# One store from four partitions, two engines for the last copy, and the last 64 KB of a weight spread by row counts of 123, 3 and 2

## The chip, the cores and the metric

The kernel runs on one core of one Trainium2 chip. The metric is the device time of one execution in microseconds (us). Most executions of one kernel lie within 0.3% of each other, which here is 0.6 us.

## The reference, cut to what matters

```python
# B=4 batches, one new token, D=512; 32 query heads over 8 key/value heads, head size 128, window 4096
q = x @ wq
o = softmax(q k^T / sqrt(128)) v        # over the last 4096 cached keys of each batch and head
a = o.reshape(4, 1, 4096) @ wo          # wo: 4096 x 512
b = ((relu(x W_gate)) * (x W_up)) @ W_down
return g * a + (1 - g) * b              # g = sigmoid(sum(x * gate_w)); result 4 x 1 x 512, bf16
```

Some 81 MB are read (key and value caches 67 MB, weights the rest) for a result of 4 KB. The order of the loads is q weights, caches, gate and up weights, the last value block, down weight, and last the output weight `wo` (4 MB).

## The kernel before

Everything is loaded by DMAs (transfers by the core's 16 DMA engines) issued from SyncE (SP). TensorE (PE) multiplies matrices and leaves its sums in PSUM; VectorE (DVE) and ScalarE (ACT) copy and work element by element. A "set" is one of the eight blocks of keys and values. The output weight comes in six pieces; `wo` row 32p+i lies in partition p, so piece (lo, hi) is a 128-row load with (hi-lo) KB in each partition. The two 256-column halves ("column tiles", j) of the result are accumulated in partitions 0-3 and 64-67 of one PSUM bank.

```python
WO_PIECES = ((0, 8), (8, 16), (16, 24), (24, 28), (28, 30), (30, 32))
OUTT = 2; OW = 512 // OUTT; OR = 128 // OUTT          # 2 tiles, 256 columns, 64 partitions apart
...
def store(E, e, t):                                   # t=0 on SP, t=1 on ACT
    E.op(lambda: e.dma_start(out...[:, OW * t:OW * t + OW], osum[OR * t:OR * t + 4, :]), waits=[("OSUM",)], ...)
...
def OQ(g):          # once after set 4, once at the end: folds the attention output into oq
    ...             # 16 matmuls of 128 columns
def WO(p):
    lo, hi = WO_PIECES[p]
    for i in range(lo, hi):
        for j in range(OUTT):
            mm(banks[ACC][OR * j:OR * j + 4, 0:OW], oq[:, i, :], Wo[:, i, OW * j:OW * j + OW], ...)
...
def FIN():          # DVE alone, both halves in one copy of 128 partitions
    E.op(lambda: v.tensor_copy(osum[:, :], banks[ACC][:, 0:OW]), ev=("OSUM",), waits=[last piece done])
```

Of the kernel before, what the change touches and what calls it, by code (L numbers as in the profile page):

```python
# [19 lines left out]
NSET = 8  # L20
# [3 lines left out]
BIG = 1.0e30  # L24
WO_PIECES = ((0, 8), (8, 16), (16, 24), (24, 28), (28, 30), (30, 32))
OUTT = 2
OW = 512 // OUTT
OR = 128 // OUTT

class _Plan:  # L30
# [71 lines left out]
def _alloc(nc, ctx):  # L102
    R = {}

    def sb(name, shape, dt):
        R[name] = ctx.enter_context(nc.sbuf_tensor(name, shape, dt))

    sb("slots", [128, NSLOT, 16384], BF16)
    sb("kt", [128, 4, 4096], BF16)
    sb("sc", [128, 2048], BF16)  # L110
    sb("pe", [128, 2048], BF16)
    sb("pT", [128, 2, 2048], BF16)
    sb("qblk", [128, NSET, 2, 144, 2], BF16)
    sb("xsb", [4, 512], BF16)
    sb("xT", [128, 16], BF16)
    sb("gwT", [128, 4], BF16)
    sb("osb", [128, 4, 512], BF16)
    sb("oq", [128, 32, 4], BF16)
    sb("identb", [128, 128], BF16)
    sb("identf", [128, 128], FP32)  # L120
    sb("ones", [128, 128], FP32)
    sb("ee", [16, 128], FP32)
    sb("e4", [16, 128], FP32)
    sb("rfold", [128, 128], FP32)
    sb("grpb", [128, 128], BF16)
    sb("own8", [128, 8], FP32)
    sb("scl", [128, 8], FP32)
    sb("maskl", [128, 128], BF16)
    sb("maskr", [128, 512], BF16)
    sb("maskf", [128, 512], BF16)  # L130
    sb("gwB", [128, 4, 128], BF16)
    sb("fold", [128, 4, 4, 64], BF16)
    sb("mx4", [128, 4], FP32)
    sb("rd32", [128, 8, 4], BF16)
    sb("negmax", [128, 2], FP32)
    sb("rowsum", [128, NSET], FP32)
    sb("recip", [128, 2, 4], FP32)
    sb("ge", [128, 2, 4], FP32)
    sb("gp", [128, 2, 4], FP32)
    sb("gg", [128, 2, 4], FP32)  # L140
    sb("hg", [128, 14, 4], BF16)
    sb("osum", [128, OW], BF16)
    R["psum"] = ctx.enter_context(nc.psum_tensor("bank", [128, 8, 512], FP32))
    return R


def _order():
    o = [("CONST", k) for k in ("mask", "grp", "rfold")] + [("XT",), ("Z",), ("Q",), ("QT",), ("KT", 0, 0), ("KT", 0, 1), ("SC", 0, 0)]
    o += [("KT", 0, 2), ("SC", 0, 1), ("KT", 0, 3), ("SC", 0, 2)]
    for s in range(1, NSET):  # L150
        o += [("KT", s, 0), ("SC", s - 1, 3)] + [("RS", 0), ("OQ", 0)] * (s == 5) + [("SW", s - 1)]
        o += [("KT", s, 1), ("PT", s - 1), ("SC", s, 0), ("KT", s, 2), ("SC", s, 1), ("KT", s, 3)]
        o += [("SC", s, 2)] + [("PV", s - 1)] * (s < NSET - 1)
    s = NSET - 1
    o += [("SC", s, 3), ("SW", s), ("PV", s - 1), ("PT", s), ("RS", 1), ("GU",), ("PV", s), ("FFN",), ("OQ", 1)]
    return o + [("WO", p) for p in range(len(WO_PIECES))]

# [29 lines left out]
def _program(nc, plan, R, aps):  # L187
# [19 lines left out]
    Wd = slot("wd")[:, 0:14 * 512]  # L207
    Wo = slot("wo", 0).rearrange("p (i c) -> p i c", i=32)
    grelu, hrow, hT = sc[:, 0:448], sc[:, 512:960], sc[:, 1024:1472]
# [28 lines left out]
    def sc_free(key):  # L238
        n = scf[key] - NSC
        return [("E",) + sck[n]] if n >= 0 else [("INIT",)]  # L240

    def set_of(s):
        return s % 4, s // 4

    def ob(s):
        return banks[OB[s % 2]]

    def store(E, e, t):
        E.op(lambda: e.dma_start(out.rearrange("b o d -> (b o) d")[:, OW * t:OW * t + OW], osum[OR * t:OR * t + 4, :]),
             ev=("OUT", t), waits=[("OSUM",)], ctr=f"d_out{t}")  # L250

    def sync(e):
# [5 lines left out]
        for it in _dma_order():  # L258
# [15 lines left out]
            elif k == "wo":  # L274
                lo, hi = WO_PIECES[it[1]]
                load(("WO", it[1]), f"d_wo{it[1]}", Wo[:, lo:hi, :], A_wo.rearrange("(p i) c -> p i c", i=32)[:, lo:hi, :],
                     waits=w)
            else:
# [3 lines left out]
                     waits=w)  # L282
        for t in range(0, OUTT, 2):
            store(E, e, t)
        E.wait([("OUT", t) for t in range(OUTT)])

# [29 lines left out]
    def tensor(t):  # L316
# [77 lines left out]

        def OQ(g):
            key = ("OQ", g)
            r = 64 * g
            for t in range(2):
                for cc in range(2):
                    for c in range(4):  # L400
                        x = 256 * t + 128 * cc + 32 * c
                        first, lastmm = (t, cc, c) == (0, 0, 0), (t, cc, c) == (1, 1, 3)
                        mm(banks[tr(key)][r:r + 64, 0:128], R["fold"][:, 2 * cc + t, c, :], osb[:, :, x:x + 32], first,
                           lastmm, ev=key if lastmm else None, pos=(0, r),
                           waits=tr_free(key) + [("NORM", 4 * g + 3), ("FOLD", 7)] if first else ())

# [18 lines left out]
        def WO(p):  # L425
            lo, hi = WO_PIECES[p]
            w = [("WO", p)] + [("E", "OQ", g) for g in range(2)]
            for i in range(lo, hi):
                for j in range(OUTT):
                    mm(banks[ACC][OR * j:OR * j + 4, 0:OW], oq[:, i, :], Wo[:, i, OW * j:OW * j + OW], False, i == 31,  # L430
                       ev=("WOP", p) if (i, j) == (hi - 1, OUTT - 1) else None, waits=w if (i, j) == (lo, 0) else (),
                       pos=(0, OR * j))

# [6 lines left out]
    for it in order:  # L440
# [27 lines left out]
        elif k == "PV":  # L468
            act.append(("NORM", it[1]))
        elif k == "OQ":  # L470
            dve.append(("EOQ", it[1]))
    dve.append(("FIN",))

    def qd(n):
# [8 lines left out]
    def vector(v):  # L483
# [62 lines left out]
        def ERS(g):  # L546
            key = ("RS", g)
            E.op(lambda: v.reciprocal(recip[:, 0, :], banks[tr(key)][:, 0:4]), ev=("E",) + key, waits=[key])
            E.op(lambda: v.tensor_tensor(recip[:, 1, :], recip[:, 0, :], gg[:, 0, :], ALU.mult), ev=("RG", g),
                 waits=[("E",) + key, ("G",)])  # L550

        def EOQ(g):
            key = ("OQ", g)
            r = slice(64 * g, 64 * g + 64)
            E.op(lambda: v.tensor_tensor(oq[r, :, :].rearrange("p i b -> p b i"),  # L555
                                         banks[tr(key)][r, 0:128].rearrange("p (b i) -> p b i", b=4),
                                         bc(recip[r, 1, :].unsqueeze(2), 2, 32), ALU.mult), ev=("E",) + key,
                 waits=[key, ("RG", g)])

# [15 lines left out]
        def FIN():  # L575
            E.op(lambda: v.tensor_copy(osum[:, :], banks[ACC][:, 0:OW]), ev=("OSUM",), waits=[("WOP", len(WO_PIECES) - 1)])  # L576

# [5 lines left out]
    def scalar(a):  # L583
# [17 lines left out]
        def NORM(s):  # L601
            E.op(lambda: a.activation(osb[:, s % 4, :], ob(s), ACTF.Copy), ev=("NORM", s),  # L602
                 waits=[("PV", s)] + ([("OQ", 0)] if s >= 4 else []))

# [14 lines left out]

        fns = dict(ECONST=ECONST, GWB=GWB, EQ=EQ, GE=GE, RELU=RELU, EXP=EXP, NORM=NORM)  # L620
        for it in act:
            fns[it[0]](*it[1:])
        for t in range(1, OUTT, 2):
            store(E, a, t)

# [29 lines left out]
```

## Time and profile before

| | before |
|---|---|
| median time | 197.36 us (197.16 to 197.44, 3 runs) |
| span of the profiled run | 195.59 us |
| bytes read, share of the 16 DMA engines in use | 81.01 MB, 97.1% |
| last piece of `wo` landed | 192.84 us after the span's start |
| last matmul ended, DVE copy ended | 193.27, 193.74 |
| stores issued / landed | 193.77 (both) / 194.94 (SP), 195.13 (ACT) |

From the page of the kernel before: the DMA queues with packets, MB and the share of 16 engines' span. Queue q1 carries the kernel's loads; the two "instruction" queues fetch the program itself.

```profile
q1 hardware_dynamic: 3904, 81.01, 97.1%
q8 instruction: 6, 0.10, 0.2%
q14 instruction: 1, 0.01, 0.0%
```

The loads alone fill the span, and the engines' work before the tail is hidden behind them. What is left is the tail. The chain that ended last, of the kernel before, in order of time (start, duration, what):

```profile
173.35 19.49 DMA slots<-in_A_wo_dram
192.84 0.04 issue
192.89 0.40 PE bank L320 x4
193.29 0.02 issue
193.31 0.42 DVE osum L576
```

The last piece lands at 192.84; after it come four matmuls, a DVE copy and the stores. The timeline of the kernel before shows the end (start, duration, engine, line, operation; in brackets the idle time before it and what ended it):

```profile
192.89 0.38 PE L320 MATMUL bank<-slots,oq 128*4 128x256 bf16 x4 [0.24 <-DMA slots<-in_A_wo_dram]
193.31 0.42 DVE L576 CAST osum<-bank 128x256 bf16<-128x256 f32 x1 [6.46 <-PE bank L320]
193.77 0.29 SPq L249 DMA_DIRECT2D out_dram<-osum  x1
193.77 0.62 ACTq L249 DMA_DIRECT2D out_dram<-osum  x1
```

One more thing must be read, and no summary line shows it. A 16-engine DMA adds 1 to its semaphore for each engine that has finished its share, so the trace holds 16 completion times for every load. For the kernel before, sorted, and split where the sorted list has its gap:

```
load ending near    early engines   late engines   last early, last late completion (us)
   51.5                  15              1
   70.9                  14              2
   80.6                  13              3
  119.5                  12              4
  148.6                  11              5
  183.4                  10              6          184.00, 185.34
  191.0 (last piece)     10              6          191.55, 192.84
16 KB instruction packets start at: 39.08, 72.01, 110.93, 146.00, 182.58 (and 191.52); an 8 KB one at 63.71
```

(A load is named by its first completion.) The number of late engines goes up by one after each instruction packet, except the last (191.52), behind which no more of the loads come.

The packet times show the delay themselves. A 16 KB packet takes 0.92 to 1.06 us, the 8 KB one 0.31 us. Behind each of the six before 191 us, a packet of a load begins 7 to 16 ns before the end of the instruction packet and is slow: 1.71 to 1.87 us for 32 KB instead of 1.21, and in the last case 0.81 us for 8 KB instead of 0.31. The packet and the slowness behind it make a delay of 1.4 to 1.6 us for each 16 KB and of 0.97 us for the 8 KB (sums from these times). The late engines stay behind to the end (the first of them 0.87 us after the last early one in the last piece): every load gives each engine the same share again. All 16 engines must finish a load, so the six late ones set the end: 192.84, where ten engines were done by 191.55. The Trainium skill, "Runtime: NRT & Kernel Launch", section "Instruction fetch mechanics", says that an engine's program is refilled in blocks of 16 KiB by DMA; the packets of 16384 bytes agree, the one of 8192 bytes is left unexplained.

### The profile page before, as it was taken

How to read it: one execution, taken by the hardware profiler on the slowest of the kernel's cores; microseconds unless marked ns; L12 is line 12 of the kernel's file. 1: busy time of each engine (PE TensorE's matmuls, PEld its weight loads, DVE VectorE, ACT ScalarE, POOL GpSimd, SP SyncE). 2: the span in 40 equal slices, each digit the busy share in tenths (PEclk: the TensorE clock that was granted, in tenths of full speed). 3: DMA queues.
4: the chain of work that ended last, by engine and by line, in shares of the span. 5: the costliest groups of instructions: out<-in, count | busy, mean ns of one | idle time of the engine just before them, and what ended most of it. 6: DMA issues, size and time to landing. Idle time of an engine off the chain costs nothing.

```text
span 195.6 us, 1780 instructions
## 1 busy us (share of the span) xinstructions
PE 121.2 (62%) x741; PEld 50.9 (26%) x741; DVE 124.0 (63%) x153; ACT 27.3 (14%) x33; POOL 9.5 (5%) x25
## 2 busy tenths in 40 slices
PE   0418279465933894595468953893395557734954
PEld 0213123122411331142113521241141112412631
DVE  6104769999299819971998199819972997460000
ACT  2213000040130013001300131014001400420100
POOL 7830000000000000000000000000000000000000
PEclk9999957999999697999886999699999789997999
DMA  6999999999999999999999999999999999999991
GB/s 221 442 423 436 429 442 436 419 436 429 436 456 429 437 426 436 429 429 429 436 429 436 426 429 429 429 429 429 429 426 429 429 405 434 448 429 403 417 402 53
DMA packets 3919, 81.12 MB, mean 415 GB/s; under 512 B 572, under 2 KB 584, under 8 KB 968
## 3 DMA queue, kind: packets, MB, share of 16 engines
q1 hardware_dynamic: 3904, 81.01, 97.1%
q8 instruction: 6, 0.10, 0.2%
q14 instruction: 1, 0.01, 0.0%
q10 hardware_dynamic: 8, 0.00, 0.0%
HBM read 81.01 MB, written 0.00 MB: 414 GB/s over the span
## 4 chain that ended last, share of the span: by engine, by line
DMA 54%; DVE 30%; PE 9%; issue 5%; SPq 1%; ACT 0%
DMA slots<-in_A_k_cache_dram 38%; DVE kt L492 21%; DMA slots<-in_A_wo_dram 10%; PE bank L320 7%; DMA gwT<-in_gate_w_dram 6%; DVE sc L528 5%; DVE qblk L518 1%; SPq L256 1%; DVE pT L543 1%; PE bank L324 1%; DVE rd L532 1%; ACT gwB L598 0%; DVE negmax L538 0%; DVE oq L555 0%; DVE osum L576 0%
## 5 line engine op out<-in xcount | busy, mean ns | idle before, releaser
L492 DVE STREAM_TRANSPOSE kt<-slots 128x2048 f32<-128x2048 f32 x32 | 73.7, 2304 | 27.5 <-DMA slots<-in_A_k_cache_dram 27.5
L320 PE MATMUL bank<-kt,qblk 128*128 128x512 bf16 x256 | 71.4, 430 | 29.2 <-DVE kt L492 29.1
L320 PEld LDWEIGHTS bank<-kt,qblk 128*128 128x128 bf16 x256 | 24.9, 106 | 70.7 <-DVE kt L492 37.6
L320 PE MATMUL bank<-slots,pT 128*64 128x512 bf16 x256 | 32.0, 407 | 5.7 <-DMA slots<-in_A_v_cache_dram 5.7
L617 ACT ACTIVATE pe<-sc,negmax 128x2048 bf16<-128x2048 bf16 x8 | 16.0, 2002 | 60.3 <-DVE negmax L538 60.3
L528 DVE CUSTOM_DVE_ANT_0 sc<-bank,maskf 128x512 bf16<-128x512 f32 x32 | 21.1, 658 | 4.1 <-PE bank L320 4.1
L320 PEld LDWEIGHTS bank<-slots,pT 128*64 128x64 bf16 x256 | 15.0, 117 | 23.1 <-issue 13.1
L543 DVE STREAM_TRANSPOSE pT<-pe 128x2048 bf16<-128x2048 bf16 x8 | 18.5, 2312 | 2.2 <-ACT pe L617 2.2
L602 ACT ACTIVATE osb<-bank 128x512 bf16<-128x512 f32 x8 | 4.8, 597 | 81.5 <-PE bank L320 81.5
L320 PE MATMUL bank<-rd,grpb 128*128 128x32 bf16 x8 | 1.5, 192 | 21.0 <-DVE rd L532 19.3
L555 DVE TENSOR_TENSOR oq<-bank,recip 64x128 bf16<-64x128 f32 x2 | 0.9, 442 | 11.5 <-PE bank L320 11.4
L320 PEld LDWEIGHTS bank<-rd,grpb 128*128 128x128 bf16 x8 | 0.8, 97 | 24.7 <-DVE rd L532 22.7
L320 PE MATMUL bank<-slots,oq 128*4 128x256 bf16 x64 | 4.3, 272 | 2.6 <-DMA slots<-in_A_wo_dram 1.9
L496 DVE COPY xT<-bank 128x16 bf16<-128x16 bf16 x1 | 0.2, 167 | 8.2 <-PE bank L324 8.2
L320 PE MATMUL bank<-slots,xT 128*4 128x512 bf16 (+1 forms) x64 | 5.2, 483 | 0.0
L576 DVE CAST osum<-bank 128x256 bf16<-128x256 f32 x1 | 0.4, 425 | 6.5 <-PE bank L320 6.5
L518 DVE TENSOR_SCALAR qblk<-bank 32x64 uint32<-32x64 uint32 x16 | 2.9, 215 | 2.3 <-PE bank L324 2.2
L320 PE MATMUL bank<-maskr,maskl 128*128 128x512 bf16 x1 | 0.6, 609 | 5.9 <-POOL maskr L296 5.9
L324 PE MATMUL bank<-identb,xsb 4*128 4x4 bf16 x4 | 0.3, 166 | 5.4 <-DMA xsb<-in_A_x_dram 5.4
L320 PEld LDWEIGHTS bank<-slots,oq 128*4 128x4 bf16 x64 | 2.3, 83 | 4.4 <-DMA slots<-in_A_wo_dram 3.1
L296 POOL TENSOR_SCALAR_AFFINE_SELECT fold<-fold 128x256 bf16<-128x256 bf16 x8 | 3.3, 417 | 1.1
L487 DVE MEMSET qblk<- 128x2304 uint32 x1 | 2.0, 1978 | 1.4 <-PEq L640 1.4
(58 smaller groups left out, 42.2 us busy)
## 6 DMA issues: line engine op xcount, KB each, us to landing
slots<-in_A_k_cache_dram SPq DMA_DIRECT2D x8, 4096.0 KB, 25.2
slots<-in_A_v_cache_dram SPq DMA_DIRECT2D x8, 4096.0 KB, 30.6
slots<-in_A_wq_dram SPq DMA_DIRECT2D x1, 4096.0 KB, 12.4
slots<-in_A_wo_dram SPq DMA_DIRECT2D x3, 1024.0 KB, 16.4
slots<-in_B_W_gate_dram SPq DMA_DIRECT2D x1, 1792.0 KB, 19.7
slots<-in_B_W_up_dram SPq DMA_DIRECT2D x1, 1792.0 KB, 23.6
slots<-in_B_W_down_dram SPq DMA_DIRECT2D x1, 1792.0 KB, 18.6
slots<-in_A_wo_dram SPq DMA_DIRECT2D x1, 512.0 KB, 19.2
```

The lines of the kernel that those rows point to most:

```text
L256: E.op(lambda: e.dma_start(dst, src), ev=ev, waits=waits, ctr=ctr)
L296: op(lambda: e.affine_select(dst, src, pattern, cmp, fill, base=base, channel_multiplier=mult), ev)
L320: E.op(lambda: t.matmul(out_, lhsT, rhs, start=start, stop=stop, tile_position=pos, skip_group_check=True), ev=ev, waits=waits)
L324: E.op(lambda: t.transpose(out_, in_, idn), ev=ev, waits=waits)
L487: E.op(lambda: v.memset(qblk[:, :, :, :, :].rearrange("p s h c e -> p (s h c e)"), 0.0), ev=("QZ",))
L492: E.op(lambda: v.transpose(kt[:, f, :].bitcast(FP32), slot("k", s)[:, 4096 * f:4096 * f + 4096].bitcast(FP32)), ev=("E", "KT", s, f), waits=w)
L518: E.op(lambda dst=dst, r=r, g=g: v.tensor_scalar(dst, src[r, g, 0:B, :, :], 0, None, op0=ALU.bitwise_or), ev=("E",) + keys[1] if (q, g) == ...
L528: E.op(lambda: v.tensor_tensor_reduce(sc[:, 512 * f:512 * f + 512], banks[scb(key)], R["maskf"][:, :], 1.0, -3.0e38, ALU.add, ALU.max, mx4 ...
L532: E.op(lambda: v.tensor_tensor(rd32[:, :, :], bc(R["own8"][:, :].unsqueeze(2), 2, 4), bc(mx4[:, :].unsqueeze(1), 1, 8), ALU.mult), ev=("MA ...
L543: E.op(lambda: v.transpose(pT[:, s % 2, :], pe[:, :]), ev=("E", "PT", s), waits=[("EXP", s)] + ([("PV", s - 2)] if s >= 2 else []))
L602: E.op(lambda: a.activation(osb[:, s % 4, :], ob(s), ACTF.Copy), ev=("NORM", s), waits=[("PV", s)] + ([("OQ", 0)] if s >= 4 else []))
L617: E.op(lambda: a.activation(pe[:, :], sc[:, :], ACTF.Exp, bias=negmax[:, s % 2:s % 2 + 1], scale=SCALE, accum_out=rowsum[:, s:s + 1]), ev= ...
```

## The change

The intent: take work off the tail. (1) The last 64 KB of `wo` (one of 64 half-rows of 512 bytes per partition) are loaded as three row groups of 123, 3 and 2 partitions. The Trainium skill, "DMA: Bandwidth & Descriptors", section "Why a DMA increments its semaphore by 16 and not by 1", says that a DMA runs on the largest number k of engines, up to 16, that divides its slowest dimension, and on the lowest-numbered k. So 123 = 3 x 41 rows go to engines 0 to 2, and so do the 3; the 2 rows go to engines 0 and 1. (2) ACT copies the first half of the result while DVE copies the second, both into partitions 0 to 3, and one store from SP replaces two. (3) The two OQ halves are merged into one at the end. (Two small constant matmuls also become bf16.)

```diff
-WO_PIECES = ((0, 8), (8, 16), (16, 24), (24, 28), (28, 30), (30, 32))
+WO_PIECES = ((0, 16), (16, 32), (32, 48), (48, 56), (56, 60), (60, 63), (63, 64))     # now in half-rows
+LOW3 = (0, 123, 126, 128)
...
-    sb("osb", [128, 4, 512], BF16)
+    sb("osb", [128, NSET, 512], BF16)
-    sb("osum", [128, OW], BF16)
+    sb("osum", [4, 512], BF16)
...
-        o += ... [("RS", 0), ("OQ", 0)] * (s == 5) ...        # OQ in two halves
+        o += ... [("RS", 0)] * (s == 5) ...                   # OQ once, at the end, 16 matmuls of 256 columns
...
-        store(E, e, t)                                         # one on SP, one on ACT
+        load(("OUT",), "d_out", out..., osum[:, :], waits=[("OSUM", 0), ("OSUM", 1)])
...
+    def wo_rows(p):
+        return [slice(a, b) for a, b in zip(LOW3, LOW3[1:])] if p == len(WO_PIECES) - 1 else [slice(0, 128)]
+                for n, r in enumerate(wo_rows(it[1])):
+                    load(("WO", it[1], n), f"d_wo{it[1]}", Wo[r, OW * lo:OW * hi], wo[r, OW * lo:OW * hi], waits=w)
...
         def FIN():     # DVE
-            v.tensor_copy(osum[:, :], banks[ACC][:, 0:OW])     # after the last piece
+            v.tensor_copy(osum[:, OW:2 * OW], banks[ACC][OR:OR + 4, 0:OW])        # after the last piece
+        def FIN():     # ACT
+            a.activation(osum[:, 0:OW], banks[ACC][0:4, 0:OW], ACTF.Copy)         # after the last but one
```

More of the change, by code (lines that the diff above doesn't have):

```diff
@@ L121, in _alloc @@
     sb("ones", [128, 128], FP32)
-    sb("ee", [16, 128], FP32)
-    sb("e4", [16, 128], FP32)
+    sb("ee", [16, 128], BF16)
+    sb("e4", [16, 128], BF16)
     sb("rfold", [128, 128], FP32)
@@ L136, in _alloc @@
     sb("rowsum", [128, NSET], FP32)
-    sb("recip", [128, 2, 4], FP32)
+    sb("recip", [128, 4, 4], FP32)
     sb("ge", [128, 2, 4], FP32)
@@ L150, in _order @@
     for s in range(1, NSET):
-        o += [("KT", s, 0), ("SC", s - 1, 3)] + [("RS", 0), ("OQ", 0)] * (s == 5) + [("SW", s - 1)]
+        o += [("KT", s, 0), ("SC", s - 1, 3)] + [("RS", 0)] * (s == 5) + [("SW", s - 1)]
         o += [("KT", s, 1), ("PT", s - 1), ("SC", s, 0), ("KT", s, 2), ("SC", s, 1), ("KT", s, 3)]
@@ L154, in _order @@
     s = NSET - 1
-    o += [("SC", s, 3), ("SW", s), ("PV", s - 1), ("PT", s), ("RS", 1), ("GU",), ("PV", s), ("FFN",), ("OQ", 1)]
+    o += [("SC", s, 3), ("SW", s), ("PV", s - 1), ("PT", s), ("RS", 1), ("GU",), ("PV", s), ("FFN",), ("OQ",)]
     return o + [("WO", p) for p in range(len(WO_PIECES))]
@@ L207, in _program @@
     Wd = slot("wd")[:, 0:14 * 512]
-    Wo = slot("wo", 0).rearrange("p (i c) -> p i c", i=32)
+    Wo = slot("wo", 0)
     grelu, hrow, hT = sc[:, 0:448], sc[:, 512:960], sc[:, 1024:1472]
@@ L246, in ob @@
         return banks[OB[s % 2]]
-    def store(E, e, t):
-        E.op(lambda: e.dma_start(out.rearrange("b o d -> (b o) d")[:, OW * t:OW * t + OW], osum[OR * t:OR * t + 4, :]),
-             ev=("OUT", t), waits=[("OSUM",)], ctr=f"d_out{t}")
     def sync(e):
@@ L275, in sync @@
                 lo, hi = WO_PIECES[it[1]]
-                load(("WO", it[1]), f"d_wo{it[1]}", Wo[:, lo:hi, :], A_wo.rearrange("(p i) c -> p i c", i=32)[:, lo:hi, :],
-                     waits=w)
+                wo = A_wo.rearrange("(p i) c -> p (i c)", i=32)
+                for n, r in enumerate(wo_rows(it[1])):
+                    load(("WO", it[1], n), f"d_wo{it[1]}", Wo[r, OW * lo:OW * hi], wo[r, OW * lo:OW * hi], waits=w)
             else:
@@ L282, in sync @@
                      waits=w)
-        for t in range(0, OUTT, 2):
-            store(E, e, t)
-        E.wait([("OUT", t) for t in range(OUTT)])
+        load(("OUT",), "d_out", out.rearrange("b o d -> (b o) d"), osum[:, :], waits=[("OSUM", 0), ("OSUM", 1)])
+        E.wait([("OUT",)])
     def gpsimd(e):
@@ L393, in PV, with OQ @@
                        (f, c) in ((3, 12), (3, 14)), ev=("PV", s) if (f, c) == (3, 14) else None, waits=w, pos=(0, r))
-        def OQ(g):
-            key = ("OQ", g)
-            r = 64 * g
+        def OQ():
+            key = ("OQ",)
             for t in range(2):
@@ L402, in OQ @@
                         first, lastmm = (t, cc, c) == (0, 0, 0), (t, cc, c) == (1, 1, 3)
-                        mm(banks[tr(key)][r:r + 64, 0:128], R["fold"][:, 2 * cc + t, c, :], osb[:, :, x:x + 32], first,
-                           lastmm, ev=key if lastmm else None, pos=(0, r),
-                           waits=tr_free(key) + [("NORM", 4 * g + 3), ("FOLD", 7)] if first else ())
+                        mm(banks[tr(key)][0:64, 0:256], R["fold"][:, 2 * cc + t, c, :], osb[:, :, x:x + 32], first, lastmm,
+                           ev=key if lastmm else None, pos=(0, 0),
+                           waits=tr_free(key) + [("NORM", NSET - 1), ("FOLD", 7)] if first else ())
         def GU():
@@ L426, in WO @@
             lo, hi = WO_PIECES[p]
-            w = [("WO", p)] + [("E", "OQ", g) for g in range(2)]
-            for i in range(lo, hi):
-                for j in range(OUTT):
-                    mm(banks[ACC][OR * j:OR * j + 4, 0:OW], oq[:, i, :], Wo[:, i, OW * j:OW * j + OW], False, i == 31,
-                       ev=("WOP", p) if (i, j) == (hi - 1, OUTT - 1) else None, waits=w if (i, j) == (lo, 0) else (),
-                       pos=(0, OR * j))
+            w = [("WO", p, n) for n in range(len(wo_rows(p)))] + [("E", "OQ")]
+            for x in range(lo, hi):
+                i, j = x // OUTT, x % OUTT
+                mm(banks[ACC][OR * j:OR * j + 4, 0:OW], oq[:, i, :], Wo[:, OW * x:OW * x + OW], False, i == 31,
+                   ev=("WOP", p) if x == hi - 1 else None, waits=w if x == lo else (), pos=(0, OR * j))
         fns = dict(CONST=CONST, XT=XT, Z=Z, Q=Q, QT=QT, SC=SC, PV=PV, SW=SW, RS=RS, OQ=OQ, WO=WO, GU=GU, FFN=FFN)
@@ L470, in _program @@
         elif k == "OQ":
-            dve.append(("EOQ", it[1]))
+            dve.append(("EOQ",))
     dve.append(("FIN",))
+    act.append(("FIN",))
     def qd(n):
@@ L547, in ERS, with EOQ @@
             key = ("RS", g)
-            E.op(lambda: v.reciprocal(recip[:, 0, :], banks[tr(key)][:, 0:4]), ev=("E",) + key, waits=[key])
-            E.op(lambda: v.tensor_tensor(recip[:, 1, :], recip[:, 0, :], gg[:, 0, :], ALU.mult), ev=("RG", g),
+            E.op(lambda: v.reciprocal(recip[:, 2 * g, :], banks[tr(key)][:, 0:4]), ev=("E",) + key, waits=[key])
+            E.op(lambda: v.tensor_tensor(recip[:, 2 * g + 1, :], recip[:, 2 * g, :], gg[:, 0, :], ALU.mult), ev=("RG", g),
                  waits=[("E",) + key, ("G",)])
-        def EOQ(g):
-            key = ("OQ", g)
-            r = slice(64 * g, 64 * g + 64)
-            E.op(lambda: v.tensor_tensor(oq[r, :, :].rearrange("p i b -> p b i"),
-                                         banks[tr(key)][r, 0:128].rearrange("p (b i) -> p b i", b=4),
-                                         bc(recip[r, 1, :].unsqueeze(2), 2, 32), ALU.mult), ev=("E",) + key,
-                 waits=[key, ("RG", g)])
+        def EOQ():
+            key = ("OQ",)
+            for g in range(2):
+                r = slice(64 * g, 64 * g + 64)
+                E.op(lambda g=g, r=r: v.tensor_tensor(
+                    oq[r, :, :].rearrange("p i b -> p b i"),
+                    banks[tr(key)][0:64, 128 * g:128 * g + 128].rearrange("p (b i) -> p b i", b=4),
+                    bc(recip[0:64, 2 * g + 1, :].unsqueeze(2), 2, 32), ALU.mult), ev=("E",) + key if g else None,
+                    waits=[key, ("RG", 1)])
         def H():
@@ L575, in FIN @@
         def FIN():
-            E.op(lambda: v.tensor_copy(osum[:, :], banks[ACC][:, 0:OW]), ev=("OSUM",), waits=[("WOP", len(WO_PIECES) - 1)])
+            E.op(lambda: v.tensor_copy(osum[:, OW:2 * OW], banks[ACC][OR:OR + 4, 0:OW]), ev=("OSUM", 1),
+                 waits=[("WOP", len(WO_PIECES) - 1)])
         fns = dict(INIT=INIT, EKT=EKT, EXT=EXT, EQ=EQ, G=G, EQT=EQT, ESC=ESC, MAX=MAX, ESW=ESW, EPT=EPT, ERS=ERS, EOQ=EOQ, H=H,
@@ L601, in NORM @@
         def NORM(s):
-            E.op(lambda: a.activation(osb[:, s % 4, :], ob(s), ACTF.Copy), ev=("NORM", s),
-                 waits=[("PV", s)] + ([("OQ", 0)] if s >= 4 else []))
+            E.op(lambda: a.activation(osb[:, s, :], ob(s), ACTF.Copy), ev=("NORM", s),
+                 waits=[("PV", s)])
         def GE():
@@ L618, in EXP @@
                                       accum_out=rowsum[:, s:s + 1]), ev=("EXP", s), waits=w)
-        fns = dict(ECONST=ECONST, GWB=GWB, EQ=EQ, GE=GE, RELU=RELU, EXP=EXP, NORM=NORM)
+        def FIN():
+            E.op(lambda: a.activation(osum[:, 0:OW], banks[ACC][0:4, 0:OW], ACTF.Copy), ev=("OSUM", 0),
+                 waits=[("WOP", len(WO_PIECES) - 2)])
+        fns = dict(ECONST=ECONST, GWB=GWB, EQ=EQ, GE=GE, RELU=RELU, EXP=EXP, NORM=NORM, FIN=FIN)
         for it in act:
             fns[it[0]](*it[1:])
-        for t in range(1, OUTT, 2):
-            store(E, a, t)
     return [("tensor", tensor), ("vector", vector), ("scalar", scalar), ("gpsimd", gpsimd), ("sync", sync)]
```

## The prediction

> **What bounds the kernel.** The load stream. The page gives the SP queue 97.1% of 16 DMA engines over the 195.6 us span. I chained the trace's DMA packets, each to the one that ended where it starts: from 1.8 us to the last weight piece no engine idles for want of an issue; a 32 KB packet takes 1.21 us. The waits of the queue on DVE and PE (160 us) cost nothing.
>
> The tail is therefore the last landing plus what follows. The chain of waits and the timeline show: last piece of output weights landed 192.84, four matmuls 192.89 to 193.29 (0.40), DVE copy 0.42, two stores issued 193.77, landed 194.94 (SP) and 195.13 (ACT), end 195.6.
>
> The last landing is not even over the engines. The 16 completions of the last piece fall into ten at 190.98 to 191.55 and six at 192.42 to 192.84. In the chained packets the six late engines are those that carried an instruction fetch among the loads (five of 16 KB, 0.92 to 1.06 us each, one of 8 KB). The four engines that carried the four rows of x, the lowest-numbered, are all early: their data ended at 190.52 to 191.02, the latest engine's at 192.37.
>
> **What the change does.** The Trainium skill, "DMA: Bandwidth & Descriptors", section "Why a DMA increments its semaphore by 16 and not by 1", says a DMA uses the largest k up to 16 that divides its row counts, on the lowest-numbered k engines. The trace agrees for x: four rows, four packets. So rows of 123, 3 and 2 go to engines 0-2, 0-2 and 0-1: the last 64 KB leaves the late engines and goes to early ones.
> - Late engines: 4 KB less each. Eight 2 KB packets at 80 ns take 0.64 us, so 4 KB is 0.16 us. Last common landing 192.84 -> 192.68.
> - Engines 0-2: some 43 packets of 512 B. The stores' 512 B packets took 25 to 32 ns, so an estimate of 1.0 to 1.2 us, less the 0.16: they end at 191.4 to 192.0, still before the late ones (192.2). No new wait.
> - PE: the piece before and the last one are then both there; three plus one matmuls, the same 0.40 us.
> - FIN: ACT copies the first half after the last but one piece, beside DVE; DVE's 0.42 us stays the one on the path.
> - One store from SP in place of two: the end follows the SP landing, not the ACT's 0.19 us later; 1 KB packets (46 ns) cost 0.02.
> - Merged OQ: 16 matmuls of 256 columns (estimate 1.75 us against 1.08) and two DVE operations of 0.44: oq is ready 1.1 us later, near 188.0; two 1 MB pieces (1.9 us of PE) then end near 189.9, before the third lands (190.34). Slack 0.4 us, no cost.
> - bf16 constants, the OQ work near 115 us, larger osb: off the DMA path, 0.
>
> Sum: -0.16 - 0.17 = about -0.33 us.
>
> **Predicted: 197.0 us, range 196.6 to 197.5.** Faster by over 2%: 0.01; within 2%: 0.98; slower: 0.01.
>
> **Right or wrong, in the profile.** Completions of the last-but-one piece end near 192.7; the last piece's 8 engine completions end before that; no ACT store; PE's last four matmuls back to back; DVE copy ends near 193.55; span near 195.25; PE waits for DMA, not for oq, before the third piece.
>
> **What would make it wrong.** An instruction fetch that falls on engine 0, 1 or 2: +1 us there, +0.7 us in all. 512 B loads far slower than the 512 B stores (above 32 ns). The ACT copy colliding with PE's last matmul in the same PSUM bank. oq over 0.4 us later than reckoned.

## The result, and the profile after

| | before | after |
|---|---|---|
| median | 197.35 us (197.16 to 197.55, 6 runs) | 197.13 us (197.06 to 197.34, 6 runs) |
| ratio of the fast runs | | 0.9991, 95% interval 0.9978 to 1.0003: the same |
| the changed kernel again, other rounds | 197.43 us (9 runs) | 197.12 us (5 runs), ratio 0.9985 (0.9972 to 0.9999) |
| span of the profiled run | 195.59 | 195.34 |

A ratio is the mean time of one kernel's fast runs over that of the other's of the same rounds, so it is not quite the ratio of the medians. The result is inside the predicted range, and "within 2%" was right; the gain is 0.22 us (0.31 in the other rounds) where the sum of the prediction was 0.33.

The page of the changed kernel, DMA queues:

```profile
q1 hardware_dynamic: 4040, 81.01, 97.1%
q8 instruction: 5, 0.08, 0.2%
q14 instruction: 1, 0.01, 0.0%
```

The same bytes, the same 97.1%. The chain that ended last, changed kernel:

```profile
174.15 18.54 DMA slots<-in_A_wo_dram
192.70 0.04 issue
192.74 0.43 PE bank L321 x4
193.17 0.02 issue
193.19 0.42 DVE osum L578
```

And its timeline:

```profile
189.04 4.08 PE L321 MATMUL bank<-slots,oq 128*4 128x256 bf16 x64 [1.07 <-DVE oq L556]
192.30 0.09 PEld L321 LDWEIGHTS bank<-slots,oq 128*4 128x4 bf16 x4 [0.33 <-DMA slots<-in_A_wo_dram]
192.74 0.14 PEld L321 LDWEIGHTS bank<-slots,oq 128*4 128x4 bf16 x4 [0.34 <-DMA slots<-in_A_wo_dram]
193.16 0.37 ACT L624 ACTIVATE osum<-bank 4x256 bf16<-4x256 f32 x1 [8.03 <-PE bank L321]
193.19 0.42 DVE L578 CAST osum<-bank 4x256 bf16<-4x256 f32 x1 [4.29 <-PE bank L321]
193.70 0.27 SPq L257 DMA_DIRECT2D out_dram<-osum  x1
```

The wait for `wo` ends at 192.70 instead of 192.84, four matmuls and a 0.42 us copy follow as before, the two copies lie side by side, and there is one store. The completions of the last two pieces of the changed kernel:

```
piece (60, 63), 16 engines: 10 early 190.78 to 191.36; 6 late 192.52 192.54 192.56 192.58 192.67 192.70
piece (63, 64), 3+3+2 completions: 192.21 192.32 192.38 192.39 192.49 192.57 192.68 192.75
store: landed 194.94
```

Eight completions for the last piece, as the rule for k asks (3 + 3 + 2); three more updates of this semaphore come when the loads are issued (175.10, 185.31, 186.71) and are left out. From event to event, in us, the difference of the two spans is:

| step | before | after | difference |
|---|---|---|---|
| last completion that the last matmul needs | 192.84 | 192.75 | -0.09 |
| from there to the end of the last matmul | 0.43 | 0.37 | -0.06 |
| to DVE's start | 0.04 | 0.07 | +0.03 |
| DVE copy | 0.43 | 0.42 | -0.01 |
| DVE's end to the store's issue | 0.03 | 0.09 | +0.06 |
| issue to the last store's landing | 1.36 (ACT) | 1.24 (SP) | -0.12 |
| landing to the span's end | 0.46 | 0.40 | -0.06 |
| sum | | | -0.25 |

The terms are 0.1 us or less, and the first of them depends on when the stream of loads happened to end in that execution. Hence the experiments.

### The profile page after: what moved, and what is told of

Its sections match the earlier page's. It is cut to its first block, busy times and chain, and to the rows that moved or that the text cites. A ratio compares the mean times of both kernels' runs of the same rounds, so it can differ in the third digit from the quotient of the medians.

```text
span 195.3 us, 1747 instructions
## 1 busy us (share of the span) xinstructions
PE 122.6 (63%) x723; PEld 51.1 (26%) x723; DVE 124.4 (64%) x153; ACT 27.5 (14%) x34; POOL 9.5 (5%) x25
## 3 DMA queue, kind: packets, MB, share of 16 engines
q1 hardware_dynamic: 4040, 81.01, 97.1%
## 4 chain that ended last, share of the span: by engine, by line
DMA 53%; DVE 30%; PE 9%; issue 5%; SPq 1%; ACT 0%
DMA slots<-in_A_k_cache_dram 37%; DVE kt L492 21%; DMA slots<-in_A_wo_dram 9%; PE bank L321 8%; DMA gwT<-in_gate_w_dram 6%; DVE sc L528 5%; DVE qblk L518 1%; PE bank L325 1%; SPq L257 1%; DVE pT L543 1%; DVE rd L532 1%; DVE negmax L538 0%; ACT gwB L601 0%; DVE osum L578 0%; DVE mx L528 0%
## 5 line engine op out<-in xcount | busy, mean ns | idle before, releaser
L321 PE MATMUL bank<-kt,qblk 128*128 128x512 bf16 x256 | 72.6, 434 | 30.9 <-DVE kt L492 30.8
L321 PE MATMUL bank<-slots,pT 128*64 128x512 bf16 x256 | 33.1, 417 | 4.8 <-DMA slots<-in_A_v_cache_dram 4.8
```

The source lines that it names most:

```text
L321: E.op(lambda: t.matmul(out_, lhsT, rhs, start=start, stop=stop, tile_position=pos, skip_group_check=True), ev=ev, waits=waits)
```

## The experiments

**Theory.** The six late engines set the end of the stream; moving 4 KB from each of them to engines 0 to 2, which are early, brings the end forward by some 0.15 us; the single store gives the rest; merging OQ costs nothing. **Rivals:** all the gain is the store's; or all is noise; or the low engines are not early; or the merged OQ eats part of the gain.

**How they are read.** The stream's end itself scatters. In the profiles below the last completion of the last 16-engine piece that all of these kernels share (up to half-row 63, in e9 up to 62.5; in `before`, its last piece) fell anywhere from 192.67 to 193.22 us, which is more than the whole gain. What is steady is the time *from that completion to the span's end*. It is the last column, and the main measure. In two rows the first column stands at another point of the stream: in `before` each engine has by then carried 4 KB more (worth 0.17 us, by e1), in e9 2 KB less (half of that). Put on the footing of the others, `before` has about 2.92 and e9 about 2.54 (estimates). Where "chained packets" are named: the trace gives each DMA packet's start, duration and size, but not its engine; on one engine the next packet starts 3 to 4 ns before the recorded end of the last, so packets can be chained. That is a reconstruction of mine, and where two engines end within a few ns it can confuse them; the completions are plain records. Times in us; "low" is the last completion of the last 64 KB (96 KB in e9).

| run | last late 16-engine completion | low, last | last matmul ends | DVE copy ends | store issued | span | span less first column |
|---|---|---|---|---|---|---|---|
| before | 192.84 | - | 193.27 | 193.74 | 193.77 | 195.59 | 2.75 |
| after | 192.70 | 192.75 | 193.12 | 193.61 | 193.70 | 195.34 | 2.64 |
| e11_same (after again) | 192.71 | 192.77 | 193.14 | 193.62 | 193.72 | 195.35 | 2.64 |
| e1_all16 | 192.77 | 192.94 (all 16) | 193.25 | 193.71 | 193.80 | 195.45 | 2.68 |
| e2_two_stores | 192.67 | 192.38 | 193.09 | 193.59 | 193.62 | 195.42 | 2.75 |
| e3_low4 | 192.82 | 193.07 | 193.38 | 193.84 | 193.93 | 195.57 | 2.75 |
| e4_small_first | 192.79 | 192.27 | 193.22 | 193.70 | 193.80 | 195.43 | 2.64 |
| e5_one_engine | 192.81 | 194.53 | 194.84 | 195.30 | 195.39 | 197.02 | 4.21 |
| e6_oq_split | 192.96 | 192.81 | 193.38 | 193.87 | 193.96 | 195.61 | 2.65 |
| e7_oq_twice | 192.98 | 192.44 | 194.48 | 194.97 | 195.06 | 196.69 | 3.71 |
| e9_best | 192.76 | 192.91 | 193.23 | 193.72 | 193.75 | 195.38 | 2.62 |
| e10_waits | 193.22 | 192.83 | 193.65 | 194.13 | 194.16 | 195.80 | 2.58 |
| e12_both | 192.83 | 192.31 | 193.26 | 193.74 | 193.77 | 195.41 | 2.58 |

Each edit below is against the changed kernel.

### e11_same: the changed kernel once more

> The changed kernel itself once more, in the same rounds as the two above, for their comparison and for what the tail's events scatter by from one execution to another. Expected: median 197.1 to 197.25; completions of the last but one piece 192.65 to 192.80; low completions up to 192.75, the last one 0.05 us after the late engines' within 0.1.

Measured: median 197.12 us (5 runs), ratio to before 0.9985 (0.9972 to 0.9999). Its profile repeats the first one: 192.71, 192.77, and 2.64. The measure repeats to 0.01 us here.

### e1_all16: the last 64 KB over all 16 engines

```diff
-LOW3 = (0, 123, 126, 128)
+LOW3 = (0, 128)
```

> The changed kernel with the last 64 KB again in one load of 128 rows over all 16 engines; all else kept. Theory (the late engines set the last landing, the low rows take 4 KB from each): last landing back from 192.75 to about 192.84 to 192.90, 0.1 us later than the changed kernel; span +0.10, time near 197.23. Rival (the low rows gain nothing, since their own eighth completion, at 192.75, is the last; all the gain is the single store): no difference, or a gain, as one load has one completion to wait for, time 197.1. Rival 2 (the whole difference is noise): 197.1 to 197.4 with no shift of the last landing in the profile.

Measured: 197.19 us (6 runs), ratio 0.9991 (0.9979 to 1.0003). The extra share costs the late engines 0.17 us (192.77 to 192.94), about the expected 0.16. But the span's end comes only 2.68 after the first column, against 2.64. The timeline of this run shows why (only the lines from the copies on, and the last weight loads):

```profile
192.81 0.25 PEld L321 LDWEIGHTS bank<-slots,oq 128*4 128x4 bf16 x4 [0.36 <-DMA slots<-in_A_wo_dram]
193.29 0.42 DVE L578 CAST osum<-bank 4x256 bf16<-4x256 f32 x1 [4.12 <-PE bank L321]
```

Three of the last four matmuls start in the 0.17 us between the two landings (192.82, 192.82 and 192.93), so that only one starts after the last (192.94 to 193.25, 0.31 us; in the changed kernel all four follow the last late completion, 192.70 to 193.12, 0.42 us). So the row groups do take 0.17 us from the landing, as the theory has it, and give back 0.11 to 0.13 of it, because nothing is computed in that time any more. Their own worth, beside an ordinary small last piece, is 0.04 us. The rival "the low rows gain nothing" is nearly right; what the row groups and the smaller last piece share is the gain over the old 256 KB last piece. That gain is a remainder, not a run of its own: of the 0.28 us from `before` (2.92) to the changed kernel (2.64), 0.11 is the new end (e2, next) and 0.04 the row groups, which leaves some 0.13 for the smaller last piece. No run brought the old piece back. By time alone e1 cannot be told from the changed kernel.

### e2_two_stores: DVE alone and two stores, as before

```diff
-    sb("osum", [4, 512], BF16)
+    sb("osum", [128, OW], BF16)
-        load(("OUT",), "d_out", out..., osum[:, :], waits=[("OSUM", 0), ("OSUM", 1)])
+        store(E, e, 0)              # and store(E, a, 1) at the end of ACT's program
-            v.tensor_copy(osum[:, OW:2 * OW], banks[ACC][OR:OR + 4, 0:OW])
+            v.tensor_copy(osum[:, :], banks[ACC][:, 0:OW])                 # ACT's copy removed
```

> The changed kernel with the end of before: DVE alone copies both halves, SP and ACT store one half each; the low rows kept. Theory: the end follows the ACT store's landing, about 1.36 us after issue, against 1.24 for the single one, but issue comes some 0.05 us sooner: time +0.10 to +0.15 us, 197.25. Rival (all the gain is the store): +0.22, as slow as before, 197.35. Rival 3 (all the gain is the low rows): 197.13, no change.

Measured: 197.24 us (5 runs), ratio 0.999 (0.9977 to 1.0003), about 0.1 us over the changed kernel, within the scatter. The measure is 2.75 against 2.64: the new end is worth 0.11 us. In this profile:

```profile
193.16 0.43 DVE L581 CAST osum<-bank 128x256 bf16<-128x256 f32 x1 [4.13 <-PE bank L325]
193.62 0.27 SPq L254 DMA_DIRECT2D out_dram<-osum  x1
193.62 0.60 ACTq L254 DMA_DIRECT2D out_dram<-osum  x1
```

The stores are issued 0.03 us after the copy (0.09 in the changed kernel), SP's lands at 194.78 and ACT's at 194.96. So ACT's store does come 0.18 us later than SP's, as in the kernel before (0.19), but the single store gives back a part of this: it waits for two engines and is issued 0.06 us later after the copy.

### e10_waits: the store's two waits in the other order

```diff
-waits=[("OSUM", 0), ("OSUM", 1)])      # ACT, DVE
+waits=[("OSUM", 1), ("OSUM", 0)])
```

> The changed kernel with the two waits of the store swapped, nothing else. Theory: DVE's end to the store's issue falls from 0.09 to about 0.04 us, time -0.05. Rival (the order of the waits is not kept by the instruction stream, or costs nothing): 0.09 us and 197.13 as before.

Measured: 197.19 us (5 runs), ratio 0.9988 (0.9975 to 1.0). In the trace of the changed kernel SP first passes a separate wait for DVE (at 193.637), the engine that ends last, and then the DMA instruction with the wait for ACT (193.702). Swapped, the separate wait is the one for ACT (194.078) and the DMA instruction waits for DVE itself:

```profile
193.71 0.42 DVE L578 CAST osum<-bank 4x256 bf16<-4x256 f32 x1 [4.72 <-PE bank L321]
194.16 0.27 SPq L257 DMA_DIRECT2D out_dram<-osum  x1
```

From DVE's end (194.133) to the issue (194.160) it is now 0.03 us instead of 0.09; the measure falls from 2.64 to 2.58, the same 0.06. The time does not show it: in this execution the stream ended late (193.22), and the profiled run took 197.55 us.

### e3_low4: four engines instead of three

```diff
-LOW3 = (0, 123, 126, 128)
+LOW3 = (0, 124, 128)
```

> The changed kernel with the last 64 KB in rows of 124 and 4, so four engines instead of three, 32 packets of 512 B each instead of 43. In the trace of the changed kernel the fourth engine of those that carried x, the one without low rows, is late: it carried the 8 KB fetch and its data ended at 191.98. Theory (an engine with a fetch has no slack): its 32 packets of 24 ns end near 192.75, landing near 193.3, 0.5 us later than the changed kernel, time 197.6. Rival (all four lowest engines are early, as the prediction said): the low data end near 191.65, last landing 192.70, time 197.05 to 197.1.

Measured: 197.31 us (5 runs), ratio 0.9995 (0.9983 to 1.0007). The eight completions of the two row groups, from the trace:

```
191.64 191.82 191.83 191.89 192.01 192.07    192.88 193.07
```

Three engines finish both groups by 192.07, and one comes 0.8 to 1.0 us later, about what the 8 KB packet and the one after it cost in `before` (0.97). So one of the four lowest engines is a late one, and the last matmul has to wait for it, as the profile says:

```profile
192.86 0.09 PEld L321 LDWEIGHTS bank<-slots,oq 128*4 128x4 bf16 x3 [0.42 <-DMA slots<-in_A_wo_dram]
193.11 0.08 PEld L321 LDWEIGHTS bank<-slots,oq 128*4 128x4 bf16 x1 [0.17 <-DMA slots<-in_A_wo_dram]
```

The measure is 2.75: 0.11 worse than with three engines, although each low engine carries fewer rows. The size was over-predicted (0.5 us expected for the landing, 0.32 found against 192.75) because the late engine's data began at 191.68 here, 0.3 us earlier than in the trace that the expectation came from. This run also corrects the prediction, which had all four lowest engines early.

### e5_one_engine: the last 64 KB on one engine

```diff
-LOW3 = (0, 123, 126, 128)
+LOW3 = (0, 127, 128)
```

> The changed kernel with the last 64 KB in rows of 127 and 1: one engine carries all 128 packets of 512 B (a doubling of the suspected cost, and more). Theory: 128 packets of 24 ns are 3.07 us; begun near 190.8 they end near 193.9, landing near 194.5, 1.75 us after the changed kernel's 192.75; time 198.8 to 198.9. Rival (the loads of few engines are not what ends last; the tail is the 16-engine stream): 197.2. A rival about the queue: its issue stands behind a full ring and starts late; then the first 512 B packet would come well after the engine's last 1536 B packet instead of right behind it, and the time would be over 199.5.

Measured: 198.69 us (4 runs), ratio 1.0068 (1.0054 to 1.0082), 1.5 to 1.6 us over the changed kernel; the last completion came at 194.53, as expected. In the chained packets the one engine took its 128 packets of 512 B from 190.90 to 193.92, 24 ns each, right behind its 1536 B packets.

```profile
192.85 0.09 PEld L321 LDWEIGHTS bank<-slots,oq 128*4 128x4 bf16 x3 [0.39 <-DMA slots<-in_A_wo_dram]
194.57 0.08 PEld L321 LDWEIGHTS bank<-slots,oq 128*4 128x4 bf16 x1 [1.63 <-DMA slots<-in_A_wo_dram]
```

This is the one experiment in which the time itself speaks: a load of few engines is on the path as soon as its engine runs out of slack, and its cost is packets times 24 ns. The queue rival did not come true, though it came near. The SP timeline of this run:

```profile
171.22 20.03 SPq L257 DMA_DIRECT2D slots<-in_A_wo_dram  x8
```

The load of one row that stands behind the 127 rows was stuck at issue from 174.30 for 16.95 us, until 191.25; the engine needed it only at 193.9.

### e4_small_first: the small row groups first

```diff
-LOW3 = (0, 123, 126, 128)
+LOW3 = (0, 3, 5, 128)
```

> The changed kernel with the last 64 KB in the order of 3, 2 and 123 rows. The low rows' data end at 191.91 but their last completion comes at 192.75, 0.84 us later, where a late engine's comes 0.46 us after its data. Theory (three completions in a row on one engine come about 0.1 us apart, behind each other): with the small ones first only one completion follows the data, last low completion near 192.5, and the last landing is the late engines' 192.70; time -0.05, 197.08. Rival (many 512 B writes are confirmed later, whatever the order): unchanged, 192.75 and 197.13. The issue of the load after the 123 rows took 10.2 us in the changed kernel; here nothing stands behind it, so the queue's issue should be free early.

Measured: 197.23 us (5 runs), ratio 0.9989 (0.9978 to 1.0001). The completions moved as the theory said: in the chained packets the low rows' data end at 191.71 and the last completion is at 192.27, 0.56 us later (the same 0.56 in e12_both). With the order of the change, three completions behind the last data, the lag from the end of the last 512 B packet, which needs no chain, was 0.79 to 0.94 us in the six profiles that have it (after, e2, e6, e7, e10, e11); with two completions (e3, e5) it was 0.61 to 0.63. So the low rows are done half a microsecond before the late engines. But the measure stays 2.64: PE issues three matmuls of the piece before anyway, and a wait of 0.05 us for the fourth disappears behind them. A cost that was real and had no effect. The issue is free, too: the SP timelines of e4 and of the changed kernel,

```profile
171.12 3.66 SPq L257 DMA_DIRECT2D slots<-in_A_wo_dram  x9
```

```profile
171.88 14.65 SPq L257 DMA_DIRECT2D slots<-in_A_wo_dram  x9
```

nine issues in 3.66 us against 14.65, as nothing stands behind the 123 rows. In the changed kernel the issue of the three rows took 10.16 us (174.98 to 185.14).

### e6_oq_split: OQ in two halves, as before

```diff
-[("RS", 0)] * (s == 5)
+[("RS", 0), ("OQ", 0)] * (s == 5)
-            mm(banks[tr(key)][0:64, 0:256], ..., osb[:, :, x:x + 32], ...)          # 16 matmuls of 256 columns
+            mm(banks[tr(key)][r:r + 64, 0:128], ..., osb[:, :, x:x + 32], ...)      # twice 16 of 128, r = 64 * g
```

> The changed kernel with the work between attention and output projection (OQ) in two halves as before, the first after set 4, the second at the end. Theory (merging is off the path): first output matmul near 188.0 instead of 189.04, PE idle before the third piece, but the last four matmuls at the same time; time 197.1 to 197.25, no difference. Rival (the merged OQ ate part of the gain, because PE ran behind the landings from 189 to 192): 0.1 us faster, last matmul earlier relative to the last landing.

Measured: 197.24 us (5 runs), ratio 0.9993 (0.9979 to 1.0006); measure 2.65 against 2.64. The output matmuls start at 187.82 instead of 189.04 and PE waits for landings again, to the same end:

```profile
187.82 1.91 PE L321 MATMUL bank<-slots,oq 128*4 128x256 bf16 x32 [0.63 <-DVE oq L556]
190.51 1.04 PE L321 MATMUL bank<-slots,oq 128*4 128x256 bf16 x16 [0.78 <-DMA slots<-in_A_wo_dram]
```

The merged OQ costs nothing. The instruction count goes from 1747 to 1779, and a sixth 16 KB instruction packet comes back, at 191.61, too late to hold up a load.

### e7_oq_twice: the merged OQ's matmuls run twice

```diff
+            for rep in range(2):
               for t in range(2):
                   ...
-                           ev=key if lastmm else None, pos=(0, 0),
+                           ev=key if lastmm and rep else None, pos=(0, 0),
```

> The changed kernel with the merged OQ's 16 matmuls run twice (same result): 1.9 us more before the output projection. In the changed kernel PE idles 0.33 us before the last but one group of four matmuls and 0.34 us before the last, so some 0.7 us of slack are left between OQ and the end. Theory: oq ready near 190.9, and the end moves by 1.9 less 0.7, so by 1.1 to 1.3 us; time 198.3. Rival (PE has ample slack): 197.2. Rival (no slack at all): +1.9, 199.0.

Measured: 198.42 us (4 runs), ratio 1.0052 (1.0038 to 1.0066); measure 3.71, 1.07 more than the changed kernel. The output matmuls start at 190.82 and never wait again:

```profile
189.79 0.88 DVE L557 TENSOR_TENSOR oq<-bank,recip 64x128 bf16<-64x128 f32 x2 [13.98 <-PE bank L321]
190.82 3.66 PE L321 MATMUL bank<-slots,oq 128*4 128x256 bf16 x64 [1.07 <-DVE oq L557]
```

The start of the output matmuls moved by 1.78 us (189.04 to 190.82) and the end by 1.07 us relative to the stream, so the changed kernel has some 0.7 us of slack behind OQ: enough for what the merge added, not for much more.

### e8_probe: which engine carries a fetch

```diff
+                if it == ("v", 0):
+                    for m in range(5, 16):          # loads of 5 to 15 rows, 52 to 92 bytes a row
+                        load(("PR", m), "d_probe", R["probe"][0:m, 64 * m:64 * m + 16 + 2 * m], A_wq[0:m, 0:16 + 2 * m])
```

> The changed kernel with eleven tiny loads of 5 to 15 rows, each of its own row size, after the first v block: a measurement of which engine carries an instruction fetch, since a load of m rows should go to the lowest m engines. If that is so, sizes nest: the engine with all eleven sizes also carries x's rows, and the chain of packets names every engine. Theory: engines 0, 1 and 2 carry no fetch, engine 3 carries the 8 KB one, five of the others a 16 KB one. If the fetches fall on engines 4 to 8, no choice of lowest engines above three can be better than three. Time near 197.2.

Measured: 198.97 us (one run, state unknown, 1.6 us over the kernel before in the same call). The probe disturbed what it was to measure: the GB/s of the ninth of 40 slices, where the small loads ran, fell to 314 from some 430, and the engines were spread over 2.4 us at the end (last shared 16-engine piece: first completion 191.46, last 193.85).

```profile
GB/s 219 432 420 445 465 439 439 429 314 425 439 439 454 425 422 432 432 432 425 425 439 432 422 425 445 432 445 445 425 425 415 432 398 448 443 413 410 414 363 27
```

The chained packets gave a map, but one in which the chains may have been exchanged after the probe, and which does not agree with e3 about the fourth engine. It is inconclusive, and which engines beyond the first three are free stays open. One thing it does show without chains: the eleven loads gave 110 completions (42.02 to 44.40), which is 5 + 6 + ... + 15, so each size m used m engines.

### e9_best: more bytes on the low engines, and the waits swapped

```diff
-LOW3 = (0, 123, 126, 128)
+LOW3 = (0, 3, 5, 128)
+WO_LOADS = (0, 16, 32, 48, 56, 60, 62.5, 64)      # last load 96 KB: 768 B a row
-waits=[("OSUM", 0), ("OSUM", 1)])
+waits=[("OSUM", 1), ("OSUM", 0)])
```

> The changed kernel with what the first runs taught: small row groups first (in that run the low rows' completions were done at 192.27, 0.5 us before the late engines' last), so the low engines can carry more: 96 KB in rows of 768 B instead of 64 KB in rows of 512 B; and the store's two waits swapped, so that the wait for ACT, which ends first, is the separate one and the wait for DVE sits on the DMA instruction. Theory: 2 KB less on each late engine (-0.08), low rows in time (last low completion near 192.6 against 192.7 of the late ones), store issued 0.04 us after DVE's copy instead of 0.09 (-0.05): span 195.2, time 197.0, about 0.1 us under the changed kernel. Rival (the low rows do not finish in time at 768 B): last low completion after 192.8, time 197.2 or more.

Measured: 197.15 us (5 runs), ratio 0.9985 (0.9973 to 0.9998), no better than the changed kernel in the same rounds (197.12, 0.9985). The rival was right: the last low completion came at 192.91, after the late engines' 192.76, so the low engines were now what ended last. The low engine that ended last took its 43 packets from 190.87 to 192.44, 1.57 us, where 512 B rows took 1.05 (190.86 to 191.91 in the changed kernel). The measure is 2.62, but at a first column that comes 2 KB earlier; on the footing of the others it is about 2.54 (estimate), where e12, the same edits with 64 KB, has 2.58. So half of the 0.08 us that the 2 KB were to bring may be left, in one profile each; the time does not show it.

### e12_both: small groups first and the waits swapped

```diff
-LOW3 = (0, 123, 126, 128)
+LOW3 = (0, 3, 5, 128)
-waits=[("OSUM", 0), ("OSUM", 1)])
+waits=[("OSUM", 1), ("OSUM", 0)])
```

> The changed kernel with the two edits that each did in its own profile what it should: small row groups first (64 KB in rows of 512 B, not 96 KB), and the store's waits swapped. Theory: low completions done 0.3 us or more before the late engines' last, DVE's end to the store's issue 0.03 us instead of 0.09, so 0.05 to 0.1 us under the changed kernel at an equal end of the stream: ratio to before near 0.998. As the end of the stream scattered by 0.5 us between the profiles so far, the time alone is expected to leave it unresolved: 197.0 to 197.2.

Measured: 197.15 us (196.98 to 197.52, 5 runs) against 197.29 of before, ratio 0.9994 (0.998 to 1.0007). The measure is 2.58, as with the swap alone. No version was shown to beat the changed kernel by its time.

## Why the prediction was right or wrong

- **Bound by the load stream, tail alone movable:** right. The share of the loads is 97.1% before and after.
- **Late engines are those that carried an instruction packet:** supported by the completions, in which the late count rises by one after each instruction packet before 191 us, and by the slow packets: each of them and the slowness of the packet behind it add up to 0.97 to 1.6 us. A cause in the strict sense is not shown: no run took the packets away.
- **"The four engines that carried the four rows of x ... are all early":** wrong. The chaining of packets by their times had a tie there in the trace of before: the 8 KB packet fitted one of these four as well as another engine. e3 shows that one of the four is late by about a microsecond (192.88 and 193.07 against 192.07). The conclusion held because the change uses only three; the prediction's own reasoning would have passed four. That 123 = 3 x 41 was chosen and not 124 = 4 x 31 is the point of the odd number.
- **Low rows, -0.16 for the landing:** the size is right within e1 (0.17). That the landing also moved by 0.14 between the two profiles shows nothing, as it scatters by 0.55 us. But the reason why it pays was only half seen: e1 shows that an ordinary small last piece has all but 0.04 of it (2.68 against 2.64 after the same completion), by leaving one matmul instead of four after the last landing.
- **"Completions of the last piece end before" the late engines':** wrong by 0.05 us, without effect; three completions behind one another on an engine (lag 0.79 to 0.94 us, against 0.56 for one, e4) were not reckoned with.
- **One store, -0.17:** this is the mis-sized term. It is worth 0.11 us (e2: 2.75 against 2.64). The missing 0.06 is the wait for two engines: e10 takes just that back (DVE's end to the issue 0.03 instead of 0.09, measure 2.58).
- **OQ ready near 188.0, slack 0.4, no cost:** no cost is right (e6), the times were not. The first output matmul came at 189.04, and PE ran behind the landings until 192.3; so PE did wait for oq and not, as predicted, for the third piece. I had taken the PV matmuls (probabilities times values) before it to end when they did before; in the changed kernel's profile they took 5.87 us instead of 5.02. That need not be the change's doing: in e11, the same kernel, they took 5.33, and the granted TensorE clock between 178.6 and 184.5 us was 0.75 in `before`, 0.71 in e11 and 0.61 in `after`. "oq over 0.4 us later than reckoned", which was to make the prediction wrong, came true without effect: the 0.4 was counted to the third landing, but PE catches up with the later pieces, and beyond the 1.0 us of delay some 0.7 us were still left (e7).
- **The sum:** -0.16 and -0.11 make -0.27 where -0.33 was predicted (the measure, on one footing, gives 0.28); the medians differ by 0.22 and 0.31 in two sets of rounds. The steps inside the profile are established; as a difference of times the gain is barely clear of noise (one interval includes 1.0, one does not).

## What to carry to other kernels

When a kernel is bound by its load stream, look at the 16 completion times of the last load, not only at the last: if they fall into two groups, the stream ends when the late group does, and the early group has room that an odd row count can reach, as long as none of the chosen engines is a late one. Before spending that, make the last piece small, so that little is computed after it: beside it the row groups were worth 0.04 us here. And measure a tail from a fixed event to the end (here it repeated to 0.01 us) when the event itself scatters by more than the effect; and put the wait for the engine that ends last on the DMA instruction itself.

## What the Trainium skill lacked or had wrong

- "Runtime: NRT & Kernel Launch", section "Instruction fetch mechanics", calls the cost of a 16 KiB boundary "mostly hidden". For the engine that runs the program it may be; in this kernel, which fills the DMA engines, one of the 16 is late after each refill and stays so (last piece of before: ten engines done by 191.55, six at 192.42 to 192.84). A refill packet of 16 KB took 0.92 to 1.06 us and the 32 KB packet behind it 1.71 to 1.76 instead of 1.21. No page that I looked up gives this cost to the loads.
- "DMA: Bandwidth & Descriptors", section "Issuing engines are not separate DMA queues", calls the sequencer's time to initiate a DMA "usually small relative to the DMA itself". A 3-row load behind a load with 41 packets on each of three engines took 10.16 us to issue, a 1-row load behind 127 packets on one engine 16.95 us; with the 3 and 2 rows ahead of the 123 (e4) the three issues took 0.26 to 0.31 us each. What limit was reached, the runs do not show.
- The same page, section "Why a DMA increments its semaphore by 16 and not by 1": its rule for k held in all runs (8 completions for 123+3+2 rows, 8 for 124+4, 2 for 127+1, 110 for 5 to 15 rows in e8). It does not say that completions of several short loads on one engine lag the data further: 0.79 to 0.94 us for three in a row, 0.61 to 0.63 for two, 0.56 for one.
- No page that I looked up has the cost of a DMA that waits for two engines: 0.09 us from the later engine's end to the issue if the separate wait is the later engine's, 0.03 us if it is the earlier one's.
